# Two sequence layers on one core: B turned by its transfers, narrow operations merged, an inverse that takes both imaginary products in two groups, and the last stores on another queue

## The chip, the core and the metric

The kernel runs on one core of a Trainium2 chip. The metric is the device time of one execution in microseconds (us), the median of several runs. Engines are called as in the profile: PE (matmul), PEld (its weight loads), DVE (vector), ACT (scalar activation), POOL (GpSimd) and SP (SyncE, which only issues transfers). SPq, ACTq and POOLq are their instruction queues. Each engine works its own queue in order and waits at an instruction until what it needs is there.

## The reference, cut to what matters

Two layers are computed side by side on sequences of 2048 steps with 640 channels, and put next to each other in the output.

```python
# A: a diagonal state space model, 640 complex states
dt = exp(log_dt); Lam_bar = exp(dt * Lam)
B_bar = ((Lam_bar - 1) / Lam)[:, None] * (B_re + 1j * B_im)
Bu = x @ B_bar.T                        # [2048, 640] complex
h[t] = Lam_bar * h[t - 1] + Bu[t]
a = 2 * real(h @ C.T) + x * Dskip

# B: a gated long convolution per channel
k_shift = causal convolution of k with 4 taps per channel
kv = k_shift * v
y = irfft(rfft(kv, 4096) * rfft(ssm_k, 4096))[:2048] + kv * ssm_D
b = q * y
out = concatenate([a, b], -1)
```

## The kernel before, in words

**Layer A** goes through the sequence in four chunks c of 512 steps, and through the states in five tiles j of 128. For each of these 20 pairs (numbered n = 5c + j): z multiplies the turned input xT with the turned matrix BT on PE (L368, ten matmuls of 512 columns), ze copies the result out of PSUM on ACT (L662), rin rotates it on DVE by tables of sines and cosines (three products, L379 to L381), sc runs two real scans on DVE (L388), and rout rotates back into a buffer h (again L379 to L381). There are NZ = 3 buffers z and NH = 8 buffers h. la keeps the last column of h on POOL (L397) and carry makes the next chunk's start from it (L402 to L404). p multiplies h with the scaled matrix Cs (L413) for four blocks i of 128 steps, and adds x times Dskip at the last j (L419); yo copies the sum on ACT into one of NYO = 3 buffers (L423), and yd stores it from POOL's queue (L427).

BT is made on the chip: B is loaded as it lies by SP in three pieces (B0, B1, B2; L166), bt turns its blocks on PE by a product with the identity (L336, 50 matmuls), and bte copies them into BT on ACT (L346, eight copies). x, k, v and C are turned on their way in, by transfers of SP that transpose (L360, L436 and L439, L442, L640).

**Layer B** goes through five groups G of 128 channels. tap makes k_shift by matmuls with diagonal weights (L474), kve copies it on ACT (L481), kv multiplies with v on DVE (L485), kvo and kvs store the product and load it in another layout from POOL's queue (L488, L491). The Fourier transforms are two stages of matmuls each: s1 (L497) and s2 (L511 to L514), once for the filter (s1h, s2h) and once for kv (s1k, s2k), each followed by a copy on ACT (L502, L517). s2he fills Hf, s2ke fills Xs0 and Xs1. y multiplies the spectra on DVE in three steps per half: step 0 writes Xs times the real part of Hf into Y (L524), step 1 Xs with its parts exchanged times the imaginary part into pw_x (L526), step 2 subtracts and adds the two halves of pw_x (L528, L529). inv is the first stage of the inverse, four pieces q of 16 matmuls on Y (L538 to L541), copied by zs (L545). zt turns the result by a transfer of SP (L549), fin is the last stage (L559), obe copies on ACT (L566), ob multiplies with q on DVE (L571), and od stores a group's result from POOL's queue (L574).

**Constants.** At the start POOL makes ramps (L170 to L180) and the phases of the transform (gp, L323 and L324) and of the tables (tp, L309); DVE makes masks (L194 to L204), phases of the small matrices (L209 to L216), Fi, the frequencies (L249 to L255), and from the sines the factors g2re, g2im and ng2im (num, rec and gam, L274 to L292), which scale C (ct on ACT, L300, and cs on DVE, L304). ACT makes the tables by its sine: tab for the rotations (L314, L158, L159), G for the transform (L328). warm0 and warm1 are 6 and 10 matmuls without a use for the result (L342), run ahead of and between the first bt.

**What sets the order.** All of this is written out by hand: a string ORDER lists every step in the order in which it is given out, and a name with @ takes one of the four PSUM tiles ps0 to ps3 until the step that copies it out. Each engine's queue is the sequence of its steps in that string; the dependencies between engines become waits. In SP's queue the start reads: B0, x0, B1, B2, kT0, vT0, CT0, hs0, CT1, kT1, x1, vT1. In ACT's: the three rows of parameters, the taps' load, lddsk, exp, dcol (a load, issued by ACT, L431), rr, aRM, trig1, bte0, bte1, tab0, bte2, ze0, and so on.

Of the kernel before, what the change touches and what calls it, by code (L numbers as in the profile page):

```python
# [19 lines left out]
D = 640  # L20
# [6 lines left out]
NH = 8  # L27
NPS = 4
NYO = 3
# [33 lines left out]
class Kernel:  # L63


    def __init__(self, ctx, tc, out, ins):
# [17 lines left out]
        for n in ("theta", "rho", "rr", "fr", "kf", "aph1", "cos1", "nr", "ni", "den",  # L84
                  "t0", "rden", "g2re", "g2im", "ng2im"):
            t(n, [128, NT], f32)
        t("dt_b", [128, NT])
        t("Fi", [128, NT], i32)
        t("rots", [128, NT, 2], f32)
# [5 lines left out]
        for n, k in (("r_hi", 1), ("r_lo", 1), ("bsh", 1), ("m_kk", 1), ("m_lo", 1), ("m_k1h", 1), ("m_ri", 1), ("m_k4", 2), ("ccol", 8)):  # L95
            t(n, [128, k], i32)
        t("r_mask", [128, 8])
        t("m_mask", [128, 8])
        t("r_cv", [128, 32])
# [35 lines left out]
        t("pw_x", [128, 2, 1024])  # L135
        t("Zt", [128, 16, 2, 128])
        early = self.pw_x[:].rearrange("p a n -> p (a n)").bitcast(f32).rearrange("p (n k) -> p n k", k=32)
        self.r_aph, self.m_aph, self.m_cv = (early[:, i] for i in range(3))
        self.r_ph, self.r_q16, self.m_ph = (early[:, i].bitcast(i32) for i in range(3, 6))
        self.ldt, self.lre, self.lim = (self.vec[:, NT * i:NT * i + NT] for i in range(3))  # L140
        self.zz = self.pool.tile([128, 2 * NT * D], bf16, name="zz")
        self.Zs = self.zz[:, 0:4096].rearrange("p (i h k c) -> p i h k c", i=16, h=2, k=16)
        self.Bn = self.zz[:].rearrange("p (r j d) -> p r j d", r=2, j=NT)
# [4 lines left out]
        self.tph = [q[:].rearrange("p a c -> p (a c)").bitcast(i32)[:, 512 * i:512 * i + 512] for q in (self.q0, self.q1) for i in range(2)]  # L148
        zf = self.Zt[:].rearrange("p i h b -> p (i h b)").bitcast(f32)
# [14 lines left out]
    def load_B(self, lo, hi):  # L164
        for r, ap in enumerate((self.A_B_re, self.A_B_im)):
            self.nc.sync.dma_start(out=self.Bn[:, r, lo:hi, :], in_=ap.rearrange("(j i) d -> i j d", i=128)[:, lo:hi, :])  # L166
# [7 lines left out]
    def pool_consts2(self):  # L174
        g = self.nc.gpsimd
        g.iota(self.ccol[:], pattern=[[1, 8]], base=0, channel_multiplier=0)
        g.iota(self.r_ph.rearrange("p (k r) -> p k r", r=2), pattern=[[4, 16], [0, 2]], base=1, channel_multiplier=0)
        g.iota(self.r_q16.rearrange("p (k r) -> p k r", r=2), pattern=[[0, 16], [16, 2]], base=0, channel_multiplier=0)
        g.iota(self.m_k4[:], pattern=[[32, 2]], base=1, channel_multiplier=0)
        g.iota(self.m_ph.rearrange("p (h a) -> p h a", h=2), pattern=[[0, 2], [1, 16]], base=0, channel_multiplier=0)  # L180

    def dve_consts(self):
# [6 lines left out]
        s(out=self.bsh[:], in_=self.pidx[:], scalar=19, op=ALU.logical_shift_left)  # L189
        v.tensor_tensor(out=self.ident2[:], in0=self.ident[:, 0:64], in1=self.ident[:, 64:128], op=ALU.add)  # L190

    def dve_masks(self):
        s = self.nc.vector.tensor_single_scalar
        s(out=self.r_hi[:], in_=self.pidx[:], scalar=4, op=ALU.arith_shift_right)  # L194
        s(out=self.r_lo[:], in_=self.pidx[:], scalar=15, op=ALU.bitwise_and)
        s(out=self.m_kk[:], in_=self.pidx[:], scalar=3, op=ALU.arith_shift_right)
        s(out=self.m_lo[:], in_=self.pidx[:], scalar=7, op=ALU.bitwise_and)
        s(out=self.m_k1h[:], in_=self.m_kk[:], scalar=1, op=ALU.arith_shift_right)
        s(out=self.m_k1h[:], in_=self.m_k1h[:], scalar=2, op=ALU.logical_shift_left)
        s(out=self.m_ri[:], in_=self.m_kk[:], scalar=1, op=ALU.bitwise_and)  # L200
        s(out=self.m_ri[:], in_=self.m_ri[:], scalar=4, op=ALU.logical_shift_left)
        s(out=self.r_hi[:], in_=self.r_hi[:], scalar=3, op=ALU.bitwise_and)
        for m, c in ((self.r_mask, self.r_hi), (self.m_mask, self.m_lo)):
            self.nc.vector.tensor_tensor(out=m[:], in0=self.ccol[:], in1=c[:, 0:1].to_broadcast([128, 8]), op=ALU.is_equal)  # L204

    def dve_phases(self):
        g = self.nc.vector.tensor_tensor
        s = self.nc.vector.tensor_single_scalar
        g(out=self.r_ph, in0=self.r_ph, in1=self.r_lo[:, 0:1].to_broadcast([128, 32]), op=ALU.mult)  # L209
        g(out=self.r_ph, in0=self.r_ph, in1=self.r_q16, op=ALU.add)  # L210
        s(out=self.r_ph, in_=self.r_ph, scalar=26, op=ALU.logical_shift_left)
        g(out=self.m_k4[:], in0=self.m_k4[:], in1=self.m_k1h[:, 0:1].to_broadcast([128, 2]), op=ALU.add)
        mp = self.m_ph.rearrange("p (h a) -> p h a", h=2)
        g(out=mp, in0=mp, in1=self.m_k4[:].rearrange("p (h o) -> p h o", o=1).to_broadcast([128, 2, 16]), op=ALU.mult)
        g(out=self.m_ph, in0=self.m_ph, in1=self.m_ri[:, 0:1].to_broadcast([128, 32]), op=ALU.add)
        s(out=self.m_ph, in_=self.m_ph, scalar=26, op=ALU.logical_shift_left)  # L216

    def act_RM(self):
        self.cos(self.r_cv[:], self.r_ph, self.r_aph)
        self.cos(self.m_cv, self.m_ph, self.m_aph)  # L220

    def dve_RM(self):
        v = self.nc.vector
        v.tensor_tensor(out=self.R[:], in0=self.r_cv[:].rearrange("p (k o) -> p k o", o=1).to_broadcast([128, 32, 4]),
# [38 lines left out]
    def act_sincos(self):  # L263
        a = self.nc.scalar.activation
        a(out=self.rots[:, :, 0], in_=self.Fi[:], func=ACT.Sin, scale=-SC)
        a(out=self.rots[:, :, 1], in_=self.Fi[:], func=ACT.Sin, scale=SC)
        self.cos(self.cos1[:], self.Fi[:], self.aph1[:])

    def dve_num(self):
        g = self.nc.vector  # L270
        tt = g.tensor_tensor
        lre, lim = self.lre, self.lim
        nr, ni, t0, den = (self.__dict__[n][:] for n in ("nr", "ni", "t0", "den"))
        tt(out=den, in0=lre, in1=lre, op=ALU.mult)  # L274
        tt(out=t0, in0=lim, in1=lim, op=ALU.mult)
        tt(out=den, in0=den, in1=t0, op=ALU.add)
        tt(out=nr, in0=self.rr[:], in1=self.cos1[:], op=ALU.mult)
        g.tensor_scalar_add(out=nr, in0=nr, scalar1=-1.0)
        tt(out=ni, in0=self.rr[:], in1=self.rots[:, :, 1], op=ALU.mult)

    def dve_gamma(self):
        g = self.nc.vector
        tt = g.tensor_tensor
        lre, lim = self.lre, self.lim
        nr, ni, t0, rden = (self.__dict__[n][:] for n in ("nr", "ni", "t0", "rden"))
        g.tensor_scalar_mul(out=rden, in0=rden, scalar1=2.0)
        for o, a, c, op in ((self.g2re[:], nr, ni, ALU.add), (self.g2im[:], ni, nr, ALU.subtract)):
            tt(out=o, in0=a, in1=lre, op=ALU.mult)
            tt(out=t0, in0=c, in1=lim, op=ALU.mult)
            tt(out=o, in0=o, in1=t0, op=op)  # L290
            tt(out=o, in0=o, in1=rden, op=ALU.mult)
        g.tensor_scalar_mul(out=self.ng2im[:], in0=self.g2im[:], scalar1=-1.0)  # L292
# [6 lines left out]
    def act_cs(self, j, r):  # L299
        self.nc.scalar.activation(out=self.ct[2 * (j % 2) + r], in_=self.Cs[:, 1, j, :], func=ACT.Copy,  # L300
                                  scale=(self.g2im, self.g2re)[r][:, j:j + 1])

    def dve_cs(self, j, r):
        self.nc.vector.scalar_tensor_tensor(out=self.Cs[:, r, j, :], in0=self.Cs[:, 0, j, :],  # L304
                                            scalar=(self.g2re, self.ng2im)[r][:, j:j + 1], in1=self.ct[2 * (j % 2) + r],
                                            op0=ALU.mult, op1=ALU.subtract)

    def pool_tab(self, j):
        self.nc.gpsimd.tensor_tensor(out=self.tph[j % 4], in0=self.lo[:], in1=self.Fi[:, j:j + 1].to_broadcast([128, CW]),  # L309
                                     op=ALU.mult)  # L310

    def act_tab(self, j):
        a = self.nc.scalar.activation
        a(out=self.tabs[:, j, 1, :], in_=self.tph[j % 4], func=ACT.Sin, scale=SC)  # L314
        self.cos(self.tabs[:, j, 0, :], self.tph[j % 4], self.aph[:])
# [4 lines left out]
    def pool_G(self, q):  # L320
        g = self.nc.gpsimd
        v = self.gph[:, q]
        g.iota(v, pattern=[[4, 4], [64, 128]], base=16 * q + 1, channel_multiplier=0)  # L323
        g.tensor_tensor(out=v, in0=v, in1=self.bsh[:, 0:1].to_broadcast([128, 512]).rearrange("p (a b) -> p a b", a=4), op=ALU.mult)  # L324
# [6 lines left out]
    def pe_bt(self, js, ks, ps):  # L331
        for r in range(2):
            i = 0
            for j in js:
                for k in ks:
                    self.nc.tensor.matmul(ps[:, r, 128 * i:128 * i + 128], lhsT=self.Bn[:, r, j, 128 * k:128 * k + 128],  # L336
                                          rhs=self.ident[:], start=True, stop=True)
                    i += 1

# [3 lines left out]

    def copy(self, eng, out, in_):
        if eng == "ACT":
            self.nc.scalar.copy(out=out, in_=in_)  # L346
        else:
            self.nc.vector.tensor_copy(out=out, in_=in_)

    def ev_bt(self, eng, js, ks, ps):  # L350
        n = len(js) * len(ks)
        if len(js) == 1:
            out = self.BT[:, :, ks[0]:ks[-1] + 1, 128 * js[0]:128 * js[0] + 128]
            self.copy(eng, out, ps[:, :, 0:128 * n].rearrange("p r (k n) -> p r k n", n=128))
        else:
            self.copy(eng, self.BT[:, :, ks[0], 128 * js[0]:128 * js[-1] + 128], ps[:, :, 0:128 * n])
# [488 lines left out]
```

## Time and profile before

| | |
|---|---|
| median of 3 runs | 224.75 us (224.44 to 225.74) |
| the profiled execution's own time | 224.18 us |
| its span, first to last instruction | 222.3 us |
| PE busy | 197.5 us, 89% |
| DVE busy | 200.4 us, 90% |
| ACT busy | 174.5 us, 79% |
| POOL busy | 49.0 us, 22% |
| mean granted clock of PE | 0.968 |

A busy PE in the profile is one that has a matmul in its pipe; how fast they follow each other has to be read from their starts. In lists of instructions a line gives the start in us, the duration in us, the engine with q for a queue, the line of the kernel, the operation, the tiles written and read, and the shapes. In lists of waits the numbers are us in total, how often, and the longest. A span starts at the first instruction; the execution's own time has some 1.9 us around it.

### The profile page before, as it was taken

What the parts mean: (1) busy time and instruction counts of PE and PEld (TensorE: products, weight loads), DVE (VectorE), ACT (ScalarE), POOL (GpSimd) and SP (SyncE); (2) the same over time, 40 slices, a digit from 0 to 9 for tenths busy, and PEclk for the clock granted to TensorE, in tenths of its full rate; (3) what the DMA queues carried; (4) which work ended last, traced back from release to release, by engine and by line L of the source; (5) the groups of instructions that cost most, each with busy time, mean ns of one, the idle gap of its engine ahead of it and who ended that gap; (6) DMA issues with size and microseconds to landing.
All of it is one profiled execution on the core that took longest, in us unless ns stands there. A gap on an engine that the chain in (4) does not pass through costs nothing.

```text
span 222.3 us, 5385 instructions
## 1 busy us (share of the span) xinstructions
PE 197.5 (89%) x2268; PEld 138.1 (62%) x2283; DVE 200.4 (90%) x306; ACT 174.5 (79%) x207; POOL 49.0 (22%) x76
## 2 busy tenths in 40 slices
PE   2968729396999999999999999999999999999990
PEld 0444314274747557974589944699756887797770
DVE  7489999999999999999999999999899989999720
ACT  1399998989977779899598986799988877783251
POOL 8745001400320002710022020065100122010250
PEclk9999976979999999999999999999999999999996
DMA  6999997959279938989466995278495058969265
GB/s 139 252 192 243 173 165 192 199 87 175 76 159 225 158 74 201 232 173 198 103 179 132 160 156 95 46 158 222 119 183 122 5 152 150 200 155 166 55 174 137
DMA packets 93455, 34.35 MB, mean 155 GB/s; under 512 B 89718, under 2 KB 90998, under 8 KB 93430
## 3 DMA queue, kind: packets, MB, share of 16 engines
q1 hardware_dynamic: 87840, 23.49, 56.7%
q0 software_dynamic: 2928, 10.49, 17.5%
q10 hardware_dynamic: 2662, 0.02, 0.7%
q8 instruction: 18, 0.29, 0.6%
q14 instruction: 7, 0.06, 0.1%
HBM read 9.52 MB, written 7.86 MB: 78 GB/s over the span
## 4 chain that ended last, share of the span: by engine, by line
PE 73%; ACT 17%; issue 3%; SPq 2%; DMA 2%; POOL 1%; ACTq 0%; POOLq 0%
PE ps L413 19%; PE ps L368 16%; PE ps L497 5%; PE ps L511 4%; PE ps L514 4%; PE ps L513 4%; PE ps L512 4%; PE ps L474 3%; PE ps L559 3%; ACT BT L346 2%; PE ps L541 2%; PE ps L539 2%; PE ps L540 2%; PE ps L538 2%; PE ps L419 2%
## 5 line engine op out<-in xcount | busy, mean ns | idle before, releaser
L413 PE MATMUL ps<-Cs,h 128*128 128x320 bf16 x320 | 54.6, 300 | 0.4 <-ACT As_kv L502 0.4
L368 PE MATMUL ps<-xT,BT 128*128 128x512 bf16 x185 | 47.5, 392 | 6.6 <-ACT BT L346 5.3
L388 DVE TENSOR_TENSOR_SCAN u<-rr,carry,w 128x512 bf16<-128x512 f32 x30 | 36.9, 1271 | 0.4
L368 PEld LDWEIGHTS <-BT 128*128 128x128 bf16 x200 | 19.1, 100 | 27.1 <-ACT BT L346 4.5
L413 PEld LDWEIGHTS <-h 128*128 128x128 bf16 x320 | 27.0, 98 | 13.0 <-issue 2.1
L662 ACT CAST z<-ps 128x1024 bf16<-128x1024 f32 x20 | 20.6, 1031 | 8.3 <-PE ps L368 6.8
L517 ACT CAST Hf<-ps 128x1024 bf16<-128x1024 f32 x20 | 20.6, 1036 | 3.0 <-PE ps L514 3.0
L545 ACT CAST zz<-ps 128x1024 bf16<-128x1024 f32 x20 | 20.2, 1037 | 2.4 <-PE ps L541 2.3
L502 ACT CAST As_h<-ps 128x1024 bf16<-128x1024 f32 x20 | 20.2, 1031 | 2.4 <-PE ps L497 2.4
L511 PE MATMUL ps<-As_h,Gre 128*128 128x128 bf16 x80 | 18.1, 226 | 4.5 <-ACT As_h L502 3.5
L502 ACT CAST As_kv<-ps 128x1024 bf16<-128x1024 f32 x20 | 19.9, 1027 | 2.6 <-PE ps L497 2.6
L517 ACT CAST Xs<-ps 128x1024 bf16<-128x1024 f32 x20 | 20.3, 1055 | 1.5 <-PE ps L514 1.0
L423 ACT CAST yo<-ps 128x640 bf16<-128x640 f32 x16 | 11.2, 700 | 11.3 <-PE ps L419 8.6
L427 POOL DMA_DIRECT2D out_dram<-yo x16 | 8.8, 551 | 48.4 <-ACT yo L423 48.0
L512 PEld LDWEIGHTS <-nGim 128*128 128x128 bf16 x160 | 15.9, 100 | 5.0 <-issue 4.4
L514 PE MATMUL ps<-As_h,Gre 128*128 128x128 bf16 x80 | 18.2, 227 | 0.0
L513 PE MATMUL ps<-As_h,Gim 128*128 128x128 bf16 x80 | 18.1, 226 | 0.0
L512 PE MATMUL ps<-As_h,nGim 128*128 128x128 bf16 x80 | 18.1, 226 | 0.0
L538 PE MATMUL ps<-Y,Hre 128*128 128x128 bf16 x80 | 17.5, 219 | 0.0
L539 PE MATMUL ps<-Y,nHim 128*128 128x128 bf16 x80 | 17.5, 219 | 0.0
L540 PE MATMUL ps<-Y,Him 128*128 128x128 bf16 x80 | 17.5, 219 | 0.0
L541 PE MATMUL ps<-Y,Hre 128*128 128x128 bf16 x80 | 17.5, 219 | 0.0
(151 smaller groups left out, 534.3 us busy)
## 6 DMA issues: line engine op xcount, KB each, us to landing
h_st<-in_B_ssm_k_dram SPq DMA_DIRECT2D x5, 512.0 KB, 4.2
kv_rows<-vT POOLq DMA_DIRECT2D x5, 512.0 KB, 3.8
kv_st<-kv_rows POOLq DMA_DIRECT2D x5, 512.0 KB, 6.9
out_dram<-yo POOLq DMA_DIRECT2D x16, 160.0 KB, 2.9
q<-in_B_q_dram SPq DMA_DIRECT2D x5, 512.0 KB, 7.4
out_dram<-q POOLq DMA_DIRECT2D x5, 512.0 KB, 6.3
zz<-in_A_B_re_dram SPq DMA_DIRECT2D x1, 480.0 KB
zz<-in_A_B_im_dram SPq DMA_DIRECT2D x1, 480.0 KB, 5.4
```

The lines of the kernel that those rows point to most:

```text
L368: self.nc.tensor.matmul(ps[:, r, :], lhsT=self.BT[:, r, k, j * 128:(j + 1) * 128], rhs=xT[:, k, :], start=(k == 0), stop=(k == NT - 1))
L388: self.nc.vector.tensor_tensor_scan(out=self.u[:, r, :], data0=rb, data1=self.w[:, r, :], initial=ini, op0=ALU.mult, op1=ALU.add)
L413: mm(ps[:, b, 0:320], lhsT=h[:, r, ts], rhs=self.Cs[:, r, j, c0:c0 + 320], start=(j == 0 and r == 0), stop=False)
L502: self.nc.scalar.copy(out=As[:, :, 32 * q:32 * q + 32].rearrange("p k (i r c) -> p k i r c", i=4, r=2), in_=ps[:].rearrange("p r (i k c) - ...
L511: mm(ps[:, 0, cs], lhsT=self.Gre[:, k1, :], rhs=re, start=True, stop=False)
L512: mm(ps[:, 0, cs], lhsT=self.nGim[:, k1, :], rhs=im, start=False, stop=True)
L513: mm(ps[:, 1, cs], lhsT=self.Gim[:, k1, :], rhs=re, start=True, stop=False)
L514: mm(ps[:, 1, cs], lhsT=self.Gre[:, k1, :], rhs=im, start=False, stop=True)
L517: self.nc.scalar.copy(out=dst[:, :, o:o + 512], in_=ps[:])
L538: mm(o_re, lhsT=self.Hre[:, k1, :], rhs=yre, start=True, stop=False)
L539: mm(o_re, lhsT=self.nHim[:, k1, :], rhs=yim, start=False, stop=True)
L540: mm(o_im, lhsT=self.Him[:, k1, :], rhs=yre, start=True, stop=False)
```

## The change

- **B.** The transfers turn it: ten transposing loads of 128 rows (two for each of five tiles j, called B0 to B4) write BT directly. bt, bte and the copy helpers are gone. z needs only its x and its own B tile. warm0 and warm1 become one warm of eight matmuls. SP's queue now starts: B0, x0, kT0, B1, vT0, B2, hs0, B3, CT0, CT1, B4, kT1, x1, vT1.
- **Narrow operations.** Masks, phases, num and gam are done with fewer and wider DVE operations (two shifts in one instruction, real and imaginary parts side by side); the two cosines of aRM become one pair of activations; three of POOL's four ramps for G are replaced by adding a constant per partition; a fifth buffer for tp takes away its wait for tab0. dcol is issued by ACT ahead of exp.
- **Products of spectra.** Step 1 works in place in Xs without exchanging the parts, and pw_x is gone. In groups 0, 2 and 4 (ADDED) step 2 adds and subtracts as before. In groups 1 and 3 it only subtracts; the inverse takes both imaginary products, one from Y and one from Xs, with the same weights, so a piece has 24 matmuls instead of 16. The next group's copies into Xs wait for step 2, or in those groups for inv, instead of step 1.
- **Stores.** The last chunk's four yd, and od4 in two halves of 64 columns, are issued by SP.
- **Buffers.** NH = 9, NYO = 4.
- **ORDER** is written anew as a whole.

```diff
-NH = 8
+NH = 9
-NYO = 3
+NYO = 4
...
-    def load_B(self, lo, hi):
+    def load_B(self, j):
         for r, ap in enumerate((self.A_B_re, self.A_B_im)):
-            self.nc.sync.dma_start(out=self.Bn[:, r, lo:hi, :], in_=ap.rearrange("(j i) d -> i j d", i=128)[:, lo:hi, :])
+            self.nc.sync.dma_start_transpose(out=self.BT[:, r, :, 128 * j:128 * j + 128],
+                                             in_=ap[128 * j:128 * j + 128, :].rearrange("n (k d) -> n k d", d=128))
...
     def act_RM(self):
-        self.cos(self.r_cv[:], self.r_ph, self.r_aph)
-        self.cos(self.m_cv, self.m_ph, self.m_aph)
+        self.cos(self.rm_cv, self.rm_ph, self.rm_aph)
...
     def dve_gamma(self):
...
+        tt(out=self.sq[:], in0=self.num[:, ::-1], in1=im, op=ALU.mult)
+        tt(out=self.num[:], in0=self.num[:], in1=re, op=ALU.mult)
+        tt(out=self.num[:, 0], in0=self.num[:, 0], in1=self.sq[:, 0], op=ALU.subtract)
+        tt(out=self.num[:, 1], in0=self.num[:, 1], in1=self.sq[:, 1], op=ALU.add)
+        v.scalar_tensor_tensor(out=self.g2[:, 0:2], in0=self.num[:], scalar=2.0,
+                               in1=self.rden[:].rearrange("p (o j) -> p o j", o=1).to_broadcast([128, 2, NT]), op0=ALU.mult, op1=ALU.mult)
+        v.tensor_scalar_mul(out=self.g2[:, 2], in0=self.g2[:, 0], scalar1=-1.0)
...
     def pool_G(self, q):
         g = self.nc.gpsimd
-        v = self.gph[:, q]
-        g.iota(v, pattern=[[4, 4], [64, 128]], base=16 * q + 1, channel_multiplier=0)
-        g.tensor_tensor(out=v, in0=v, in1=self.bsh[:, 0:1].to_broadcast([128, 512]).rearrange("p (a b) -> p a b", a=4), op=ALU.mult)
+        flat = lambda n: self.gph[:, n].rearrange("p a b -> p (a b)")
+        if q == 0:
+            g.iota(self.gph[:, 0], pattern=[[4, 4], [64, 128]], base=1, channel_multiplier=0)
+        g.tensor_tensor(out=flat(q), in0=flat(0), in1=self.bsh[:, q:q + 1].to_broadcast([128, 512]), op=ALU.add if q else ALU.mult)
...
         elif step == 1:
-            tt(out=cr[:], in0=Xs[:, ::-1, :], in1=self.Hf[:, 1:2, hs].to_broadcast([128, 2, 1024]), op=ALU.mult)
+            tt(out=Xs[:], in0=Xs[:], in1=self.Hf[:, 1:2, hs].to_broadcast([128, 2, 1024]), op=ALU.mult)
         else:
-            tt(out=Y[:, 0, hs], in0=Y[:, 0, hs], in1=cr[:, 0, :], op=ALU.subtract)
-            tt(out=Y[:, 1, hs], in0=Y[:, 1, hs], in1=cr[:, 1, :], op=ALU.add)
+            tt(out=Y[:, 0, hs], in0=Y[:, 0, hs], in1=Xs[:, 1, :], op=ALU.subtract)
+            if add:
+                tt(out=Y[:, 1, hs], in0=Y[:, 1, hs], in1=Xs[:, 0, :], op=ALU.add)
...
+    def pe_inv(self, q, ps, added):
         psf = ps[:].rearrange("p a n -> p (a n)")
+        x = self.__dict__[f"Xs{q // 2}"]
         for i in range(4):
             k1 = 4 * q + i
+            im = [self.Y[:, 1, 128 * k1:128 * k1 + 128]]
+            if not added:
+                im.append(x[:, 0, 128 * (k1 % 8):128 * (k1 % 8) + 128])
+            for part, (a, b) in enumerate(((self.Hre, self.nHim), (self.Him, self.Hre))):
+                terms = [(a, self.Y[:, 0, 128 * k1:128 * k1 + 128])] + [(b, v) for v in im]
+                for n, (w, v) in enumerate(terms):
+                    self.nc.tensor.matmul(psf[:, 256 * i + 128 * part:256 * i + 128 * part + 128], lhsT=w[:, k1, :], rhs=v,
+                                          start=(n == 0), stop=(n == len(terms) - 1))
...
+    def store_ob(self, eng, G, lo, hi):
+        o = D + 128 * G
+        eng.dma_start(out=self.o2[:, o + lo:o + hi].rearrange("(a b) c -> b a c", b=128), in_=self.qt(G)[:, :, lo:hi])
...
+ADDED = (0, 2, 4)
...
+B0 ldldt ldlim ldlre pc ldsk dc pc2 gp0 x0 lddsk dc2 dcol vt@0 gp1 gp2 vec exp rho Fi rr trig1 warm@1 kT0 pp dS0 tp3 num tp0
+aRM tp2 z0@1 B1 vT0 rec tab0 gam ze0 tap0_0@0 gp3 dRM tp1 tap0_1@1 tn0 tp4 dD tab1 tab3 z1@2 B2 kve0_0 tab4 kve0_1 rin0 sc0
+tn1 ze1 hs0 G0 B3 rout0 tab2 kv0_0 dS1 z2@0 had0 s1h0_3@1 tn3 s1h0_0@3 kv0_1 CT0 kvo0 rin1 ze2 sc1 G1 rout1 s1he0_3 tn4 z3@2
+s1h0_2@0 s1he0_2 s1h0_1@1 s1he0_0 CT1 tn2 s1he0_1 rin2 la0 nG1 nG0 ze3 kvs0 ct1_0 sc2 rout2 rin3 s2h0_2@1 s2h0_1@3 s2h0_3@2
...
+p3_1_2 yd3_3 p3_2_2 p3_1_3 p3_2_3 p3_1_4 yd3_0 ob4_0 ob4_1 p3_2_4 od4_0 yo3_1 od4_1 yd3_1 yo3_2 yd3_2
```

## The prediction, made before the changed kernel was built or run

> **What bounds the kernel now.** I read the page's slices first, then the busy time by stages, the waits, the chain that ended last and the instructions of the first 60 us and of the end. In the slices each digit is the busy share of 5.6 us in tenths.
>
> ```profile
> PE   2968729396999999999999999999999999999990
> DVE  7489999999999999999999999999899989999720
> ACT  1399998989977779899598986799988877783251
> PEclk9999976979999999999999999999999999999996
> ```
>
> Two engines are full for most of the span: DVE from the fourth slice on, PE from the eleventh. ACT is full in slices 3 to 7, where PE has holes and twice loses its clock. The busy time by stages (columns: PE, PEld, DVE, ACT, POOL, granted clock, DMA share, GB/s) shows the same in us.
>
> ```profile
> 30.00:36.70 6.70, 4.16 (x15) 1.44 (x16) 6.60 (x12) 6.11 (x7) 0.69 (x1) 0.55 1.13 231
> 44.00:54.50 10.50, 8.36 (x117) 6.22 (x117) 10.26 (x15) 9.49 (x12) 0.00 (x0) 0.84 0.73 121
> 60.00:209.80 149.80, 149.17 (x1844) 108.78 (x1854) 145.06 (x190) 119.65 (x132) 25.59 (x38) 1.00 0.73 150
> 209.80:216.20 6.40, 6.40 (x78) 5.21 (x76) 1.39 (x2) 4.00 (x5) 3.98 (x5) 1.00 0.53 134
> 216.20:222.30 6.10, 0.01 (x1) 0.00 (x0) 0.00 (x0) 0.69 (x1) 0.54 (x1) 0.68 0.55 143
> ```
>
> From 60 to 216.2 us PE idles 0.6 us, at full clock; DVE idles 4.7 us until 209.8, mostly in gaps of hundredths. So the middle is worth what is taken off both queues, and three things are open: when they start, how much they hold, and the 6.1 us behind PE's last matmul. The waits (us in total, times, longest) name who holds the start.
>
> ```profile
> PE ps L368 <- ACT BT L346: 5.3, 4, 2.5
> ...
> PE ps L511 <- ACT As_h L502: 3.5, 1, 3.5
> ...
> ACT rr L261 <- DMA zz<-in_A_B_re_dram: 2.8, 1, 2.8
> ...
> ACT yo L423 <- DMA out_dram<-yo: 2.5, 1, 2.5
> ```
>
> PE waits for ACT, and for the B copies most. ACT itself lost 2.8 us because dcol, a load queued on ACT between exp and rr, could not be issued until an earlier B load had landed. The last line is the copy of yo3_3, which waits for a store out of one of three yo buffers. The chain (start, us, what) has both places.
>
> ```profile
> 8.69 0.68 ACTq L431
> ...
> 12.47 1.17 ACT BT L346 x2
> ...
> 210.68 0.70 ACT yo L423
> ...
> 216.19 1.76 issue
> 217.95 0.56 POOLq L840
> ```
>
> **Part 1, ACT's start.** dcol is now ahead of exp, where ACT has nothing else to do (exp waits until 6.42). rho ends at 7.23, so rr runs at 7.25 instead of 9.41. The Sin table takes 1.28 (to 8.75, Fi is there at 8.54), the sines 0.72 as before (9.5), the merged aRM about 0.6 instead of 1.1 (10.1). Next is tab0, which needs POOL's second product tp0: 8.62 + 2 x 1.01 = 10.65. Three activations of 1.80 in all give 12.45, against 15.44 before.
>
> **Part 2, z0.** It needs x0 and the first B block. SP now issues two small turned loads ahead of x0; the nearest row is x0's own 3.23 us for four times the rows, 0.8 each. x0 goes out at 2.4 and lands 5.7 to 6.8 later (xT's range): 8.1 to 9.2, or 10.2 if it has to wait for an earlier load as dcol did. I take 9.3. z0 costs 2.13 us at full clock and 4.06 at half (z4 at 32.62, where the clock was 0.55). The warm-up matmuls started 0.43 us apart from 4.49 on and only sped up at 10.2 (the granted clock is shown as full there; I go by the spacing); the new eight end near 7.9. So I take half speed: z0 ends at 13.4, and its copy, 0.9, at 14.3 (bounds 12.4 and 15.3; before 17.25). TensorE: Matmul & The Clock Gate of the Trainium skill, Part 1, says that about 3.4 us of sustained activity release the clock; by that eight warm-ups just suffice, z0 would take 2.13, and the total would come out at most 1.9 lower. The row speaks against it: here it took 5.7 us.
>
> **Part 3, B turned by its transfers.** 50 matmuls (4.15 us busy) leave a PE that idles there, so nothing. Eight copies leave ACT: 1.17 + 0.90 + 0.27 + 1.60 + 0.92 + 0.90 = 5.8 us along its queue; 2.1 of it lay before z0's copy and is in the 14.3. ACT is then 17.25 - 14.3 = 3.0 ahead at z0's copy and 6.6 ahead once the other 3.7 are gone. Up to 54.5 us it is ACT that releases PE, so PE has its dense stretch 6.5 us earlier; 3.0 if a landing holds ACT back instead, 8.0 if z0 runs at full clock and nothing holds. On the DMA engines I count the edit at nothing: turning 524k elements (Zt) keeps SP 5.2 us, so B's 819k cost some 8 us, and its plain 1.64 MB at the 190 GB/s of this stretch took 8.6. On SP's queue kT0 moves up by about 2.5 us; B1 to B3 (1.6 each) then stand ahead of vT0, h and the two C loads, B4 ahead of kT1 and x1. By 0.8 a load CT1 ends near 27.5 instead of 25.6 and x1 near 36 instead of 34.4. Cover: CT1 is first used by ACT near 36, x1 by z6 near 50. POOL saves three iotas (0.56 each) and has its products done by 14.7.
>
> **Part 4, DVE.** Its small operations now number 11 instead of 15 from num to gam (2.4 us to 1.75). Chained from the sines at 9.5: dS0 aside, num to gam end near 12.1, dRM 13.1, tn0 13.4, diagD 1.66: first rotation at 15.0 instead of 17.29. There before lost 1.5 us beside POOL's products:
>
> ```profile
> 17.29 1.41 DVE L379 TENSOR_TENSOR rot_p<-tabs,z 128x1024 bf16<-128x1024 bf16 x1
> ...
> 18.62 1.52 DVE L380 TENSOR_TENSOR rot_x<-tabs,z 128x1024 bf16<-128x1024 bf16 x1
> ```
>
> Elsewhere these take 0.68. POOL is done by 14.7, so the scan starts at 17.1 instead of 20.91. Going on through kv0, the three tn, both nG and the next rotations I keep 3.5 us (2.0 to 4.5). Masks and phases end under the wait for vec or in the idle time before the sines: nothing. In groups 1 and 3 one addition goes from each half: 4 x 0.685 = 2.7 us off DVE. The product with Hf's imaginary part keeps its 1.22, in place.
>
> **Part 5, the inverse.** Per group 4 x 4 x 2 = 32 more matmuls, 64 in all. In the dense stretch one such matmul follows another after 0.0555 us: 3.55 us more on PE, none of it beside idle time. The weights are loaded anyway (PEld 109 of 149.8).
>
> **The two queues together.** PE's own: 216.2 - 6.5 + 3.55 = 213.25. DVE's: its last h moves by 3.5 + 2.7; behind it PE did 7.3 us and now, in the new order, 8.3 (four pieces with j = 4 and two fin, 5.1, the rest 0.54 each): 216.2 - 6.2 + 1.0 = 211.0. The later one decides: PE ends at 213.2. The ninth h and the fourth yo loosen waits of which the middle shows none: nothing there.
>
> **Part 6, the end.** Now 6.1: 0.78 for the yo buffer, 0.69 copy, 0.3 to the issue, 4.1 until the store has landed, 0.2. With four buffers and SP's queue: 0.1, 0.69, then the store. No store by SP is in the trace; bounds are the 160 KB loads by SP, 2.3, and POOL's last store, 4.1. I take the middle, 3.2, and 0.2: 4.2, so 1.9 less (0.9 to 2.8).
>
> **Sum.** 213.2 + 4.2 = 217.4 span, and 1.88 around it (224.18 less 222.3): **219.3** us against 224.18. The runs' median is 0.57 above the profiled execution, so 219.9 on that scale; I keep 219.3.
>
> **Rivals.** (a) *The start frees more*: z0 at full clock, the landings in time, SP's store at its lower bound: PE's lead 8.0, the end 3.3: 211.7 + 3.3 + 1.9 = **216.9**, and with DVE's queue deciding instead (211.0) 216.2. For it: ACT is the only thing PE waited for.
> (b) *The halved store ends last.* od4 now goes in two stores with runs of 64 elements instead of 128. od4_1 is issued about 2.3 us ahead of PE's end (4.3 of PE work stand behind fin4, copy and product take 2.0). The whole store has as many runs as each half and landed in 5.0 to 8.0; if time goes by runs, the second half queued behind the first lands 8.0 later, 5.7 behind PE's end: 213.2 + 5.9 + 1.9 = **221**. Against it: half the bytes. DMA: Bandwidth & Descriptors, Specifications, in the Trainium skill, sets 512 B as the smallest transfer at full rate, below which a write becomes read-modify-write; both sizes lie below, so it supports the count by runs.
> (c) *Slower.* The small turned loads cost like kTb's turned piece in this stretch, 2.76 each, not 0.8. Place: SP's queue ahead of CT1. Eight of them instead of six plain loads put CT1's landing at 0.7 + 3.2 + 4.2 + 2.4 + 0.6 + 9.3 + 22 + 2.8 = 45; ACT, at ct1_0 by 36, stands for 9 us, the lead of 6.5 is gone and 2.5 lost, and PE still has 3.55 more: 222.3 + 4.2 + 1.9 = **228**. It eats cover from 1.7 us a load on, and the time is slower than before from about 2.4 on. Against it: kTa's 1024 rows took 1.46 beside it.
> (d) *The start gives only DVE's 3.5* to PE as well: 216.2 - 3.5 + 3.55 + 4.2 + 1.9 = **222.4**.
>
> **Chances.** Forecast 0.56, (a) 0.17, (b) 0.10, (c) 0.07, (d) 0.10. The range reaches from 215.5, just below (a), to 222.8, just above (d), and leaves out (c) and the edges. A difference within 0.5% (1.1 us) is about what cannot be told from none here. Faster by more: 0.89; within: 0.04, from late (d); slower: 0.07, (c).
>
> **What would show it.** rr near 7.3 and tab0 done near 12.5; no L346 copies, z0's copy near 14.3; DVE's first scan near 17; PE without holes from about 48 instead of 54.5, and dense until 213; the inverse with 24 matmuls in groups 1 and 3; less than 4.5 us behind PE's end. If ACT or PE waits for CT, kT or B landings, or DVE shows holes of over 2 us in the middle, the prediction is wrong.

## The result, and the profile after

The changed kernel takes **222.41 us** (median of 4 runs, 222.37 to 222.56); the kernel before took 224.59 beside it. The ratio is 0.9893, 95% interval [0.9859, 0.9927]: 1.1% faster, where 2.2% and 219.3 us were forecast. (Three of the kernels further down had an execution or two that was disturbed; their medians leave it out.) The profiled execution took 222.40 us with a span of 220.6. Its slices, to be held against those of before:

```profile
PE   3499803979989999999999999999999999999991
DVE  3399999999999999999999999999999999999720
ACT  0659999899787678995897988669979987473342
```

PE still has its hole in slices 6 and 7 (28 to 39 us) and is full from the thirteenth on. ACT has no activation in the first slice. The same by stages (columns as before: PE, PEld, DVE, ACT, POOL, granted clock, DMA share, GB/s):

```profile
30.00:36.70 6.70, 1.01 (x16) 0.70 (x16) 6.56 (x11) 6.67 (x8) 1.19 (x1) 0.59 0.98 248
44.00:54.50 10.50, 8.80 (x134) 6.56 (x134) 10.26 (x14) 10.50 (x13) 0.00 (x0) 1.00 0.79 151
60.00:209.80 149.80, 148.61 (x1878) 110.60 (x1885) 144.37 (x188) 118.24 (x130) 26.62 (x41) 1.00 0.70 144
215.75:220.60 4.85, 0.04 (x1) 0.00 (x0) 0.00 (x0) 0.69 (x1) 0.00 (x0) 0.83 0.62 130
```

The forecast had two ends to the span: PE done at 213.2, and 4.2 us behind it. Measured are 215.8 and 4.83. Of the 3.1 us that are missing, 2.5 lie in PE's end and 0.6 behind it. The chain that ended last says where the 2.5 came from; these are its pieces at the start (start, us, what):

```profile
2.11 4.26 DMA BT<-in_A_B_im_dram
...
6.45 0.68 ACTq L403
...
7.16 1.28 ACT L256
8.46 0.22 ACT dt_b L256
```

L403 is dcol, L256 is exp with the load of its table. In the kernel before, exp and rr were these lines (L258 and L261 there):

```profile
6.42 0.21 ACT L258 ACTIVATE dt_b<-vec 128x5 bf16<-128x5 f32 x1 [0.58 <-DVE vec L241]
9.41 0.21 ACT L261 ACTIVATE rr<-rho 128x5 f32<-128x5 f32 x1 [2.78 <-DMA zz<-in_A_B_re_dram]
```

dcol, put ahead of exp, could be issued only when the second half of B0 had landed (2.11 + 4.26 = 6.37). exp ran at 8.46 instead of the 6.42 of before, rr at 8.90 instead of the forecast 7.25, and tab0 was done at 15.86, not 12.45 (before: 15.44).

**Why dcol waits there.** In the trace each load names the semaphore that it raises when it lands. SP and ACT draw them from the same eight, 100 and 102 to 108, and from the ninth load on each is issued only once the last load with the same semaphore has landed, whatever it loaded and whoever issued it:

| load (kernel) | semaphore | its last user, landed at | issued at |
|---|---|---|---|
| lddsk by ACT (after) | 102 | B0, first half, 3.88 | 3.90 |
| dcol by ACT (after) | 104 | B0, second half, 6.37 | 6.45 |
| B1 by SP (after) | 106 | x0, 10.51 | 10.53 |
| dcol by ACT (before) | 103 | B1, first half, 8.66 | 8.69 |

Just ahead of dcol, ACT's queue has an instruction of its own that waits for semaphore 104 and ends at 6.41. So dcol, needed by POOL at 23 us only, held up everything behind it on ACT's queue.

**A second loss at the same place.** The phases of the small matrices (pp) now stand behind Fi on DVE, and ran beside POOL's products for the tables and the transform (10.25 to 16.73):

```profile
10.51 0.86 DVE L213 CUSTOM_DVE_ANT_0 rot_p<-rot_p 128x128 uint16<-128x128 uint16 x1
...
12.37 0.97 DVE L215 TENSOR_SCALAR rot_p<-rot_p 128x64 int32<-128x64 int32 x1
...
14.75 1.00 DVE L270 TENSOR_TENSOR sq<-vec 128x10 f32<-128x10 f32 x1
...
16.67 0.16 DVE L272 TENSOR_TENSOR num<-trig,rr 128x10 f32<-128x10 f32 x1
```

Narrow operations take 0.16 to 0.18 us when POOL is idle (L213 0.23 in the second run of point 2 below). The first three lines here take 0.86 to 1.00, which is nearly one POOL product (1.04); the last, at the end of POOL's last product, takes 0.16. ACT waited for L215, the last of the phases (us in total, times, longest):

```profile
ACT rot_p L157 <- DVE rot_p L215: 2.3, 1, 2.3
```

The Trainium skill, page SBUF — State Buffer, section SBUF: two separate sides, says that VectorE and GpSimd share a pair of ports, and that one instruction holds it until it ends (on VectorE's side it names instructions with two inputs and those in a two-port mode). The times agree: each of the five long ones from 10.51 to 16.75 ended 0.02 to 0.08 us behind the end of a POOL product. DVE's first scan came at 21.84, not 17.1, and even later than before (20.91).

### The profile page after: what moved, and what is told of

The parts are those of the page before. It is cut to its first block, busy times and chain, and to the rows that moved or that the text cites. A ratio compares the mean times of both kernels' runs of the same rounds, so it can differ in the third digit from the quotient of the medians.

```text
span 220.6 us, 5391 instructions
## 1 busy us (share of the span) xinstructions
PE 195.3 (89%) x2278; PEld 138.6 (63%) x2289; DVE 197.3 (89%) x294; ACT 169.3 (77%) x197; POOL 41.7 (19%) x69
## 4 chain that ended last, share of the span: by engine, by line
PE 71%; ACT 14%; DVE 9%; DMA 2%; issue 1%; SPq 1%; ACTq 0%; DVEq 0%
PE ps L385 20%; PE ps L340 12%; PE ps L515 10%; PE ps L469 5%; PE ps L534 4%; PE ps L483 4%; PE ps L485 4%; PE ps L486 4%; PE ps L484 4%; PE ps L446 3%; PE ps L391 2%; DMA BT<-in_A_B_im_dram 2%; DVE Cs L298 2%; ACT As_h L474 2%; ACT z L626 2%; ACT tabs L158 2%
## 5 line engine op out<-in xcount | busy, mean ns | idle before, releaser
L385 PE MATMUL ps<-Cs,h 128*128 128x320 bf16 x320 | 53.7, 300 | 0.8 <-ACT z L626 0.8
L340 PE MATMUL ps<-xT,BT 128*128 128x512 bf16 x189 | 46.9, 390 | 4.1 <-DMA xT<-in_A_x_dram 3.1
L340 PEld LDWEIGHTS <-BT 128*128 128x128 bf16 x200 | 19.3, 100 | 26.7 <-issue 6.7
L385 PEld LDWEIGHTS <-h 128*128 128x128 bf16 x320 | 27.6, 98 | 12.2 <-issue 1.9
L515 PE MATMUL ps<-Y,Hre 128*128 128x128 bf16 x160 | 23.7, 219 | 0.0
L489 ACT CAST Hf<-ps 128x1024 bf16<-128x1024 f32 x20 | 20.0, 1024 | 4.2 <-PE ps L486 4.1
L483 PE MATMUL ps<-As_kv,Gre 128*128 128x128 bf16 x80 | 17.6, 219 | 0.5 <-ACT aph L453 0.5
L483 PEld LDWEIGHTS <-Gre 128*128 128x128 bf16 x160 | 16.1, 100 | 2.4 <-issue 1.4
```

Source lines behind the costliest of these rows:

```text
L340: self.nc.tensor.matmul(ps[:, r, :], lhsT=self.BT[:, r, k, j * 128:(j + 1) * 128], rhs=xT[:, k, :], start=(k == 0), stop=(k == NT - 1))
L385: mm(ps[:, b, 0:320], lhsT=h[:, r, ts], rhs=self.Cs[:, r, j, c0:c0 + 320], start=(j == 0 and r == 0), stop=False)
L483: mm(ps[:, 0, cs], lhsT=self.Gre[:, k1, :], rhs=re, start=True, stop=False)
L489: self.nc.scalar.copy(out=dst[:, :, o:o + 512], in_=ps[:])
L515: self.nc.tensor.matmul(psf[:, 256 * i + 128 * part:256 * i + 128 * part + 128], lhsT=w[:, k1, :], rhs=v, start=(n == 0), stop=(n == len(t ...
```

## Experiments

The ratios are to the kernel before, run beside them on the same chip; times are medians.

**1. The start: dcol behind z0's copy, phases early, and both.** The edits to the order, cut (+ is where a step stands now, - where it stood); the dependencies that guard its place go with it:

```diff
 e1: ... x0 lddsk dc2 -dcol vt@0 ... gam ze0 +dcol tap0_0@0 ...
 e2: ... lddsk dc2 +pp dcol vt@0 ... kT0 -pp dS0 ...
 e3: both
```

> The changed kernel with one step moved: dcol, the load that ACT issues, stands behind ze0 instead of ahead of exp. Theory S (the start's moves cost what the start was to gain, and DVE's queue hands on every us that its first scan moves): exp ends near 6.6 instead of 8.67, Fi near 8.5 instead of 10.16, first scan near 20.2 instead of 21.84, total 1.2 to 1.8 us less, 220.6 to 221.2. Rival P (PE's queue, with 3.55 us more matmuls, sets the middle, the start is hidden): the first scan moves, the total stays within 0.5 us of 222.4. Rival L (the landings of x0 and of the B blocks, 1.27 a load, hold z0 and what follows): exp moves, the first scan does not by more than 0.5.

> The changed kernel with pp (phases of the small matrices on DVE) ahead of vec instead of behind Fi, where its operations took 0.9 us beside POOL's products instead of 0.18. Theory S: aRM no longer waits 2.3 us on ACT, tab0 is done near 14.1 instead of 15.86, the first scan near 20.0, total 1.3 to 2.0 us less, 220.4 to 221.1. Rival P: total within 0.5 of 222.4. Rival L: first scan moves by less than 0.5.

> Both moves together. Theory S: tab0 done near 12.5, z0 still from 10.5 to 14.6 at half speed, first rotation near 16, first scan near 18, total 3 to 4 us less, 218.4 to 219.4, which is the forecast on record. Rival P: within 0.8 of 222.4. Rival L: z0 and the later B blocks hold it, total 221 to 222.

Measured: 222.13 (0.9886 [0.9863, 0.9908]), 221.85 (0.9878 [0.9845, 0.9911]) and 221.97 (0.9879 [0.9854, 0.9905]), none told apart from the changed kernel. Yet in the third the first scan came 3.5 us earlier (18.32). Laid beside the changed kernel, instruction by instruction, its DVE is 2.1 us ahead until 130 us and then waits for ACT's copies, which wait for PE, and is 0.3 ahead from 183 us on. ACT and PE are 0.65 us *behind* from 16.7 us to 57: dcol, moved down ACT's queue, now drew the semaphore of vT's load and held ACT for 4.37 us in the midst of the tables. What a lead of DVE can bring is one wait of ACT in the changed kernel, at 58 us, for DVE's scaling of C (the row holds from 50 to 62 us):

```profile
ACT Zt L294 <- DVE Cs L298: 1.3, 1, 1.3
```

In the third run this wait is gone, but ACT's own lag took most of the gain, and PE is 0.3 us ahead from 62 us on. In the profiled execution of the second, ACT is not behind: DVE's lead of 1.0 us came out whole at the end (221.37). So the theory that DVE's queue passes each us of the first scan on to the end fell here; up to that wait a lead of DVE counts, and only while ACT keeps its place.

**2. dcol off ACT's queue.** POOL has nothing to do after its last table product until h_st lands, so dcol goes there (by itself, and with the phases early):

```diff
-        self.nc.scalar.dma_start(out=self.dcol_b[0:128:16, :], ...
+        self.nc.gpsimd.dma_start(out=self.dcol_b[0:128:16, :], ...
 ... tn0 tp4 +dcol dD ...
```

> The changed kernel with dcol alone moved to POOL, behind its last table product; the phases stay late. In the changed kernel dcol could be issued at 6.45 us only, and exp's table load behind it at 7.16; with both moves the table load began at 5.15 and the time was 219.8. If dcol on ACT's queue is what cost the forecast 2 us, this gives most of them: 219.8 to 221.2. If the phases' place counts as much, as two runs with dcol still on ACT suggest (0.6 us for the phases, 0.3 for dcol), 221.5 or more.

> The run with the phases early and dcol behind the first z, but dcol issued by POOL behind its last table product, where POOL has nothing to do. In that earlier run ACT stood 4.37 us at dcol, so its tables, z1 and every ACT and TensorE instruction behind them came 0.65 us later than in the changed kernel, while DVE's scans came 2.1 to 3.5 us earlier; DVE's lead was given up at 130 to 138 us, where it caught up with TensorE's. If TensorE with ACT sets the time, freeing ACT of the 4.37 us makes this run 1 to 2.5 us faster than that one: 219.5 to 221. If DVE's queue set it, nothing more comes: 222. If the landing of the C blocks and x1 holds TensorE at 30 to 40 us anyway, nothing more either, and the idle time of TensorE there shows it.

Measured: 220.53 (0.9814 [0.9784, 0.9845]) for dcol alone and **219.76** (0.9777 [0.9719, 0.9835]) with the phases early. With dcol alone moved, exp is this line:

```profile
6.55 0.21 ACT L256 ACTIVATE dt_b<-vec 128x5 bf16<-128x5 f32 x1
```

With both, rr starts at 6.89, tab0 is done at 12.62, z0's copy at 15.22 and PE at 213.43; the forecast had 7.25, 12.45, 14.3 and 213.2. (z0's copy is 0.9 late because z0 itself ended at 14.27, not 13.4.) PE and DVE in the middle:

```profile
60.00:150.00 90.00, 90.00 (x1158) 64.58 (x1157) 87.95 (x116) 73.64 (x81) 15.73 (x27) 1.00 0.73 156
150.00:205.00 55.00, 55.00 (x690) 43.17 (x688) 52.84 (x68) 40.62 (x45) 8.55 (x11) 1.00 0.70 140
```

PE (first pair) has no idle time at all; DVE (third) has 4.2 us. All but 0.5 us of the missing time of the forecast is back, and it was in the start: 1.9 by dcol and some 0.8 by the phases, for which ACT waited.

**3. Is it the queue or the wait?** dcol stays on ACT, but changes places with lddsk:

```diff
 ... ldsk dc +dcol pc2 gp0 x0 -lddsk dc2 -dcol vt@0 ... rr trig1 +lddsk warm@1 ...
```

> The changed kernel with dcol still on ACT's queue, but issued straight behind the shift filter's loads, and the load of the skip vector moved behind the sines instead; the phases stay late. dcol's issue costs ACT its 0.68 us still. If what held ACT is that the tenth load in program order waits for the landing of an earlier one (B's second half, 6.4 us), exp is free at its data, near 6.0, and the time is that of the run with dcol alone on POOL: 220.1 to 221.3. If dcol costs by standing on ACT's queue at all, 221.8 or more.

Measured: 221.31 (0.9851 [0.9813, 0.9890]). dcol now drew the semaphore of B0's first half and was issued at 4.89; exp ran at 6.89, against 6.55 with dcol on POOL and 8.46 in the changed kernel. At exp, then, the wait is 1.6 of the 1.9 us, and dcol's own place on ACT's queue the other 0.3. The total cannot be split in this way, because lddsk met the same trap in its new place:

```profile
13.01 0.39 ACTq L161 DMA_DIRECT2D dsk_raw<-in_A_Dskip_dram  x1
13.49 0.26 ACT L157 ACTIVATE rot_p<-rot_p 128x64 f32<-128x64 int32 x1 [3.92 <-DVE diagS L431]
...
15.83 0.99 ACT L626 CAST z<-ps 128x1024 bf16<-128x1024 f32 x1
```

lddsk drew the semaphore of B1's first half, which landed at 12.99, so the activations behind it and z0's copy ran as late as in the changed kernel (13.43 and 15.77 there). Only DVE kept a lead: its first scan starts at 20.27 instead of 21.84, and ACT's wait for the scaling of C is gone. So the 1.1 us of this run came by DVE, 0.8 of it in the profiled execution (221.64 against 222.40).

**4. B turned, by itself.** The kernel before with only the ten turned loads, without bt and bte; the same with dcol on POOL; and the kernel before with only dcol on POOL:

```diff
-            self.nc.sync.dma_start(out=self.Bn[:, r, lo:hi, :], ...
+            self.nc.sync.dma_start_transpose(out=self.BT[:, r, :, 128 * j:128 * j + 128], ...
```

> The kernel before with one part of the change alone: B turned by its transfers (B0, x0, kT0, B1, vT0, B2, CT0, hs0, B3, CT1, B4 on SP), the 50 matmuls and the eight copies into BT gone, both warm-ups kept, all else and the order as before. Theory S with DVE's queue deciding: ACT is 5 us freer, but DVE's first scan can only move as far as DVE's own small operations, which ended at 17.25, allow: 0 to 1.5 us less than before. The step of the prediction (ACT releases PE, so PE's dense stretch and the end move by 5 or more): 3 to 6 us less. Rival L: the transfers come later, 0 to 3 us more than before.

> The kernel before with B turned by its transfers (which alone was 1.8 us slower), and dcol on POOL. In that slower run ACT stood 4.57 us at dcol instead of 2.78 before, and rr came at 11.21 instead of 9.41: the same 1.8 us. If the stall at dcol was the whole loss and turned B gives ACT its 5.8 us back for something, this is 2 to 4.5 us below that run: 222 to 224.4, at or below the kernel before with the same move. If the turned loads themselves are too slow on SP's queue, it stays at 225 or more.

> The kernel before, with dcol alone moved from ACT's queue to POOL, behind the table product tp2. In its trace dcol is issued at 8.69, 2.06 us after exp's end, and ACT stands 2.78 us until the rr behind it. If ACT's start sets the whole chain there too, up to 2.7 us faster: 222 to 223. If TensorE and B's turning on ACT (eight copies) hold the first scan anyway, no gain: 224 to 224.6.

Measured: 226.38 (1.0077 [1.0052, 1.0103]), 224.09 (0.9973 [0.9938, 1.0008]) and 223.56 (0.9939 [0.9914, 0.9964]). Turning alone is *slower*: dcol drew the semaphore of kT0's load there, ACT stood 4.57 us instead of 2.78, which is as much as the 1.8 lost. With dcol out of the way it is no faster than the kernel before with the same move. The waits of PE from 44 to 54.5 us in that run say why (L414 is p there, L305 the scaling of C on DVE):

```profile
PE ps L414 <- DVE Cs L305: 5.1, 1, 5.1
```

In that run PE idles 6.1 of these 10.5 us and ACT 4.8: both are early, and stand before DVE's scaling of C, whose queue is full and whose first scan (20.24) is where it was without the turned B (20.10). ACT's 5.8 us are freed, as forecast; they are worth nothing until DVE is early too. That the other parts of the change bring this is argued; no run here takes those apart. Moving dcol in the kernel before gave 1.0, not 2.1 us, and the trace shows where the rest went: the narrow DVE operations came earlier too and met POOL's products (four of 0.87 to 1.00 us), so that the first scan moved by 0.8 us only.

**5. Which queue is the bound: additions on DVE against matmuls on PE.** ADDED is the list of groups that add on DVE:

```diff
-ADDED = (0, 2, 4)
+ADDED = (0, 1, 2, 3, 4)      # e4, and on the run with dcol on POOL e10
+ADDED = (0, 2)               # e5
+ADDED = (0, 1, 2, 4)         # e16, on the run with dcol on POOL
```

> The changed kernel with all five groups adding their imaginary products on DVE, as before the change: TensorE loses 64 matmuls (3.55 us), DVE gets four additions (2.74 us). If TensorE's queue alone is the bound, 3.5 us less: 219 us. If DVE's queue alone is the bound, 2.7 us more: 225. If both are full (in the changed kernel DVE waited only 0.2 us between 42 and 190 us, TensorE had 1.2 us idle between 60 and 205), the last h comes up to 2.5 us later and the matmuls behind it shrink from 8.7 towards the 7.6 of the kernel before: 223 to 224.

> The changed kernel with the last group's imaginary products by the inverse too (groups 1, 3 and 4): TensorE gets 32 more matmuls (1.77 us), DVE loses two additions (1.37 us). TensorE the bound: 1.8 us more, 224.2. DVE the bound: 1.4 us less, 221.0. Both full: the last h up to 1.4 us earlier and TensorE's end up to 1.8 us later, so 223.5 to 224.2, since what stands behind TensorE's end stays the same.

> The same with all five groups adding on DVE: TensorE 3.55 us less, DVE 2.74 us more. If TensorE sets the time and DVE has a lead of 2 us or more by the earlier start, this is faster than the run before it by 1 to 3 us: 217.5 to 219.5. If DVE is the bound, slower by up to 2.7 us: 222 to 224.

> The run with dcol on POOL and the phases early, but with only the fourth group's imaginary products in the inverse: against that run TensorE has 1.77 us less and DVE 1.37 us more. There TensorE had no idle time at all from 54.5 to 205 us and DVE 4.3 us; with all five groups added on DVE it was TensorE that idled 2.9 us and DVE 3.4. If the two queues bound each other in this way, the halfway point is 0.3 to 1.3 us faster than both: 218.5 to 219.5. If the one or the other alone sets the time, it lies between 219.7 and 220.1.

Measured: 223.50 (0.9952 [0.9927, 0.9976]), 223.12 (0.9930 [0.9900, 0.9960]), 220.00 (0.9801 [0.9754, 0.9848]) and 219.01 (0.9762 [0.9715, 0.9809]). On the changed kernel both directions cost, 1.1 and 0.7 us (the interval of the second overlaps that of the changed kernel): both queues are full, as the last case of each expectation had it. The second came out 0.4 us below its range because what stands behind PE's end did not stay the same: in the two profiled executions PE ended 2.0 and 1.9 us later than in the changed kernel (217.75 and 217.71; exp's own delay is 0.4 and 0.1 of it), and the time behind it was 4.01 and 3.46 instead of 4.83 (Part 6 below). On the mended start the two inverse groups bring nothing that can be told from noise: with all additions on DVE PE idles 2.9 us instead, for nearly the same time. The last of the four has what halfway was to give, but see point 6. The stages with all additions on DVE and dcol on POOL, columns as before:

```profile
60.00:150.00 90.00, 89.13 (x1138) 63.65 (x1137) 88.09 (x118) 74.59 (x83) 16.12 (x27) 1.00 0.74 160
150.00:205.00 55.00, 52.96 (x641) 40.42 (x639) 53.58 (x69) 39.45 (x44) 8.53 (x11) 1.00 0.68 139
```

**6. z0's clock.** 15 warm-up matmuls instead of 8, on the run with dcol on POOL, on the changed kernel, and with one inverse group (the fourth's or the second's):

```diff
-K.pe_warm(8, ps)
+K.pe_warm(15, ps)
```

> The run with dcol on POOL and the phases early, with 15 warm-up matmuls instead of 8. There the eight ran from 4.0 to 7.6 and z0 went at half speed, 9.85 to 14.2; ACT waited 1.70 us for it. If the clock wants more work ahead of z0, z0 takes 2.2 us and its copy on ACT comes up to 1.7 earlier; TensorE, which is full from 54.5 us on in that run, can then end up to 1.7 us earlier: 218.1 to 219.5. If the landings of the C blocks and DVE's scans hold the middle, or z0 stays slow, 219.8.

> The changed kernel with 15 warm-ups and nothing else. If z0's half speed costs wherever it stands, 0.6 us faster as with dcol on POOL: 221.8. But in the changed kernel ACT came to z0's copy at 15.77, straight from the table, 1.2 us after z0's end, so z0 was not what ACT waited for: 222.2 to 222.6.

> The two last gains together: dcol on POOL, phases early, only the fourth group's imaginary products in the inverse, 15 warm-ups. The one gave 0.75 us, the other 0.62. If the one relieves TensorE's queue and the other its start, they do not overlap: 218.2 to 218.6. If both only gave z0 its full clock (the first of them had it in its profile with eight warm-ups too), 218.9 to 219.1.

> The same with the second group's imaginary products in the inverse instead of the fourth's. The queues' totals are the same, so if only totals count, the same as that run. If DVE is what is late at the end (the additions of the fourth group stand nearer to it), up to 0.7 us slower.

Measured: 219.14 (0.9766 [0.9724, 0.9808]), 222.66 (0.9928 [0.9908, 0.9947]), 219.96 (0.9790 [0.9765, 0.9815]) and 220.14 (0.9808 [0.9778, 0.9837]). z0 runs at full speed in all four: PE's instructions with 15 warm-ups and dcol on POOL (L328 the warm-ups, L340 z0), where eight gave z0 4.42 us:

```profile
3.87 4.80 PE L328 MATMUL ps<-lo,ident 128*128 128x512 bf16 x15
9.37 2.32 PE L340 MATMUL ps<-xT,BT 128*128 128x512 bf16 x10 [0.70 <-DMA xT<-in_A_x_dram]
```

In the changed kernel this brings nothing, as its own expectation said: ACT comes to z0's copy at 15.77, straight from tab0. And the gains of 0.6 and 0.75 us in two of the runs do **not** add; the run with both has neither. What sorts these executions is another thing, the start of exp in the profiled one:

| run | exp at | profiled execution's time |
|---|---|---|
| one inverse group; 15 warm-ups; both, with the second group | 5.81, 5.81, 5.80 | 219.03, 219.19, 219.02 |
| dcol on POOL; all added; both, with the fourth group | 6.45, 6.50, 6.50 | 220.04, 220.58, 220.13 |

0.7 us at exp go with 0.9 to 1.6 us at the end, whichever kernel it is. lddsk, on ACT ahead of exp, waits for the semaphore of B0's first half; in the first row that had landed by 3.82, in the second at 4.71 to 4.76. The single times of these kernels lie at 219.0 to 219.5 and at 219.8 to 220.6, and all but the one with all additions on DVE have some of both. So between them nothing was shown but, in the profiled executions, the same wait once more. The best version of this study is the changed kernel with dcol on POOL and the phases early, 2.2% under the kernel before, with or without the rest. Taking lddsk off ACT as well was not tried.

**7. The stores.** The last chunk's yd and the halves of od4 by POOL again:

```diff
-    lambda c=c, i=i: K.store_yo(nc.sync, c, i)
+    lambda c=c, i=i: K.store_yo(nc.gpsimd, c, i)
```

> The changed kernel with the last yd and od4 stores issued by POOL again. The time behind TensorE's end was 6.1 us with POOL's stores before and is 4.85 in the changed kernel. If SP's issue is what the tail gained, 1.0 to 1.5 us slower: 223.4 to 223.9. If the gain came from the shorter work ahead of the last stores, the same: 222.4.

Measured: 223.74 (0.9959 [0.9935, 0.9982]), 1.3 us more. In the profiled execution 0.4 of it is the start again (exp at 8.86, PE's end at 216.21) and 1.0 the time behind PE's end, 5.87 instead of 4.83. So SP's stores are what the tail gained.

## Why the prediction was wrong, point by point

- **Part 1 failed, and with it the size.** "dcol is now ahead of exp, where ACT has nothing else to do" took ACT's idle time for dcol's, and did not ask when dcol could be issued. The page of before already showed dcol waiting for a B load, and the prediction says so; it gave x0 such a wait as a bound in Part 2 and gave dcol none in its new place. exp came 2.0 us late. Worth 1.9 us, by the run with dcol alone moved. The rest of Part 1 was right: with dcol gone and the phases early, tab0 was done at 12.62 (forecast 12.45).
- **Part 4's "masks and phases: nothing" failed.** Behind Fi the phases met POOL's products, and three of them took 2.8 us, where such an operation takes 0.2. Worth some 0.8 us (from 220.53 to 219.76, less sure than the first, the intervals overlap). The same mechanism kept the first scan from 17.1: with both mended it starts at 19.11, six operations in the way taking 0.90 to 1.00. The saving of 2.7 us in groups 1 and 3 is borne out: the last scan starts 1.5 us earlier (205.19 to 203.69), although the first is 0.9 later, 2.4 in all.
- **Part 2** was right in its mechanism (half speed, 4.00 us) and 1.1 us early: each of the two small turned loads ahead of x0 took 1.31 us of SP, not 0.8, so x0 went out at 3.47 and landed at 10.51. It cost nothing here; ACT came later still. The clock rule of the Trainium skill (TensorE: Matmul & The Clock Gate, Part 1: released after about 3.4 us of sustained work) was weighed down by a row of before in which it took 5.7. With 15 warm-ups in a row the spacing fell from 0.43 to 0.21 us after 2.9, 3.4, 4.7 and 5.8 us in the four runs: the rule fits the first two and is too short for the others. After eight, z0 took 2.3 us in two traces and 3.7 to 4.4 in the others, so nothing should hang on eight.
- **Part 3** was right for ACT (5.8 us gone) and wrong in "up to 54.5 us it is ACT that releases PE": DVE's scaling of C stood right behind (5.1 us of PE's time in point 4, 1.3 of ACT's at 58 us in the changed kernel). PE's lead came out as 216.2 + 3.55 - 215.8 = 4.0 instead of 6.5 us; with the start mended it is 6.3.
- **Part 5**: 3.55 us on PE was right in size (384 matmuls of the inverse instead of 320, 0.056 us apart). That both queues are full was right too, so closely that moving work either way costs.
- **Part 6** gained 1.25 instead of 1.9, and a term of it was misread. The trace of before has no "4.1 until the store has landed": the last store was issued at 217.97 and landed at 220.44, 2.47 us later, and the other 1.85 us are the program's closing instructions, for which the sum has 0.2. In the changed kernel the last store took 2.60 us to land and the closing 0.90; with POOL's stores (point 7) 3.16 and 1.64. What became shorter is the wait for the yo buffer (0.78 to 0.08) and the closing; the store did not. SP's queue has a price of its own (start, us):

```profile
211.78 3.87 SPq L550 DMA_DIRECT2D out_dram<-q  x2
215.76 1.75 SPq L399 DMA_DIRECT2D out_dram<-yo  x2
```

  The second half of od4 took 2.43 us to issue. It was out of the way at 215.65, before yd3_1's copy was done (215.74), but yd3_1's issue took 1.26 us as well (two yd ahead of od4 took 0.35 each), and the last store, whose copy was done at 216.56, could be issued at 217.12 only. It landed at 219.72. Over the runs with SP's stores on the changed kernel's order the time behind PE's end goes with that issue: 4.6 to 4.9 us where od4's second half took 2.2 to 2.4, 4.0 to 4.1 where it took 1.7 to 1.8, 3.5 where it took 1.1. Why the issue takes so long is not shown.
- **The rivals.** (d) gave 222.4, the measured time, but not by what happened: DVE did not bring 3.5 us to PE; its first scan came later than before. (b) did not happen: the second half of od4 landed at 218.95, ahead of the last yd. (c) had its place right, SP's queue, and its price wrong: the ten loads took 1.2 to 1.3 each but for two of 1.7 and 2.1, 1.4 on average, below the 1.7 from which it was to eat cover. (a) did not come about even with the start mended.

## What to carry to other kernels

Of a transfer that is moved, ask first which earlier transfer must have landed before it can be issued, and then what stands behind it on its engine: in these kernels eight shared semaphores mean that a small, early and idle-looking load waits for the one eight loads ahead. Every transfer that a change adds at the start moves such a wait, so a load that nobody needs soon belongs on a queue where nobody stands behind it. And where two engines are full at the same time, a gain on one of them is worth no more than the wait that the other has for it: look at who is next before pricing it.

## What was not expected of the hardware

- A load on the queues of SP or ACT is issued behind the landing of the load with the same of eight semaphores; a load by POOL at 14.62 drew another one (111) and did not wait.
- Narrow DVE operations take 0.9 to 1.0 us instead of 0.17 while POOL runs 512-column integer products. In the kernel before, with dcol moved, this gave back half of the 2.1 us that the earlier sines had won.
- A small turned load (128 rows of 640 columns) holds SP for 1.2 to 1.3 us in eight of ten cases of the changed kernel and for 1.7 and 2.1 in the others; x0, with four times the rows, took 3.02 us.
- SP's issue of a strided store of 256 KB took 2.43 us with another like it in front, 0.38 without.
